# Block-sparse attention and a residual MLP on one core: four booked transfer times in the planner's order

## The chip, the core and the metric

The kernel runs on one core of a Trainium2 chip. The metric is the device time of one execution in microseconds (us). The version before has a median of 322.15 us in five runs (320.83 to 324.29). In the profile the engines are called PE (TensorE, matmuls), PEld (its weight loads), DVE (VectorE), ACT (ScalarE), POOL (GpSimd, here the issuer of loads) and SP (SyncE, the issuer of stores and of transposing transfers).

## What is computed

Attention over 4 batches, 8 heads, 768 positions and 64 elements a head, with a mask over blocks of 32 positions, then a residual MLP that mixes positions and then channels:

```python
scores = (q @ k.T) / sqrt(64)
mask = |bi - bj| <= 1, or block 0 or 23 on either side, or kb in sampled_blocks[qb]
attn = softmax(where(mask, scores, -1e9));  x = attn @ v      # (4, 768, 512)
a1 = alpha1 * x + beta1
u = x + lam * (w_tok @ a1)                                    # w_tok 768 x 768
a2 = alpha2 * u + beta2
out = u + lam * (relu(a2 @ w_ch1) @ w_ch2)                    # 512 -> 2048 -> 512
```

Inputs and output are float32; the kernel works in bf16 and f16 with float32 sums.

## The kernel before

**The work.** Two heads of a batch make a *pair*; there are 16, `p` = 0 to 15, four to a batch. A pair's scores are cut into nine *units* of 1024 columns. For the pairs 0 to 5 a unit is one group of QK matmuls on PE (L658), an exponential on ACT (L673) and PV matmuls (L698), with the mask inside the matmul as extra rows of q and k. For the pairs 6 to 15 two heads run side by side in QK (L736), the exponential is at L762, and VectorE applies the mask as a minimum with a table, `maskT` (L767), ahead of PV (L794). When a head's PV is complete, VectorE takes the reciprocal of the sums (L630) and multiplies (L633), which empties the PSUM bank `ops` and writes `x_sb`. For a pair follow: a1 on VectorE (L850 and L858, tile `a1p`), the position mixing on PE in two groups of 18 matmuls (L870, into PSUM tiles `mm`), its sum with x on VectorE (L880, which empties the `mm` bank), the product with alpha2 (L886, tile `ub`), and a transposition into `uT`: on PE (L907) for batch 0, by a transfer that SP issues (L917) for the others.

Once a batch's four `uT` are there, the channel part runs in eight half-batches `kk`: 16 groups of four matmuls with w_ch1 (L943, into `mm`), each with a relu on ACT (L954) or VectorE (L958) into `hts`, then three outputs of 16 matmuls with w_ch2 (L988, in groups of four, into `cp`, and near the end into `ops` too), an addition on VectorE (L1005), which empties `cp`, and a store on SP (L1012). There are two `mm` banks and, as long as attention lasts, one `cp` and one `ops`.

**Scaling of w2.** w_ch2 comes in four chunks of 512 KB (`load_w2`, L377) into `w2b`. The factor lam of the output is multiplied into it in place by eight VectorE instructions of 128x1024 (`sw`, L471), two to a chunk. Output matmuls L988 of the quarter `r` need the scalings 2r and 2r+1.

**The mask table.** VectorE makes 24 rows of it (L486), `mout` (L492) writes them out to a scratch tensor `mask_rows` in DRAM, each repeated 32 times, and `min_` (L495) reads the table back into `maskT`. Both transfers are issued on POOL, the second after the first is complete; both carry 1152 KB.

**Loads.** q, k and v of a pair are loads of 192 KB each on POOL (L308); VectorE casts q and k into `rel` (L508) and v into `vext` (L816). From pair 6 on SP then issues two transposing transfers (L597) that make `qx` and `kx`. From pair 8 on a pair's loads are held back: VectorE writes a *flag* (L324, `raise_flag`), POOL copies it (L306, `held`), and then issues q, k and v. The flag of pair p comes after the fourth unit of pair p - 2.

**What sets the order.** Each engine runs its instructions in program order, and that order is made when the program is built: a planner in the kernel holds every piece of work as a `Job` with a booked duration, a priority, dependencies and buffers taken and given. It goes through a clock of its own, gives each engine that is free the ready job of highest priority, emits its instructions, and books when it will be over. Loads leave in a fixed order by priority: those of pairs 0 to 6 with the other weights between, `mout`, two chunks of w2, `min_`, two chunks of w2, the pairs 7 to 15. A load's end is booked on one serial clock for transfers:

```python
if j.xfer is not None:
    dma_free[0] = max(dma_free[0], t + 2300.0) + j.xfer
    j.done = dma_free[0] + 200.0
```

and POOL takes no load while that clock is more than `AHEAD` = 13000 ns in front. Booked times decide the order alone; on the chip every instruction waits for what it really needs. At gaps in PE's plan before the first L988 the planner puts in matmuls on a dummy tile (L170, `keep_warm`).

Of the kernel before, what the change touches and what calls it, by code (L numbers as in the profile page):

```python
# [66 lines left out]
def kernel(  # L67
# [206 lines left out]
    def Copy(prio, fn, deps, take=(), give=()):  # L274
        j = Job(("ACT", "DVE"), 550.0, prio, fn, deps, take, give)
        j.alt = ACT_COPY
        return j
# [9 lines left out]
    def mmt(n, cols):  # L287
        return n * (max(cols, 60) / 2.4 + 2.7)
# [9 lines left out]
    def Load(xfer, prio, fn, deps=(), take=()):  # L298
        j = Job("POOL", 720.0, prio, fn, deps, take)
        j.xfer = xfer  # L300
        return j
# [12 lines left out]
    wload = {}  # L314
# [58 lines left out]
    def load_w2(g, prio, deps):  # L373
        def fn():
            if g == 0:
                w2tile.append(wk.tile([P, 16, DM], BF, name="w2b", tag="w2b", bufs=1))
            nc.gpsimd.dma_start(  # L377
                w2tile[0][:, 4 * g : 4 * g + 4, :],
                moe_w_ch2[ts(g, 4 * P), :].rearrange("(o p) n -> p o n", p=P),
            )  # L380

        wload["w2", g] = Load(2500.0, prio, fn, deps, ("w2b",) if g == 0 else ())

    order = iter(range(1000))
    load_pair(0, next(order))
# [16 lines left out]
    mout_prio = next(order)  # L402
    w2_prio = [next(order) for _ in range(2)]
    min_prio = next(order)
# [7 lines left out]
    for t in range(NT):  # L412
# [9 lines left out]
        j = Job("PE", mmt(NT, P), (5, t), tr, [wload["tok", t // 2]], take=("mm",))  # L422
# [4 lines left out]
    for g in range(4):  # L427
        load_w2(g, w2_prio[g], wtok_jobs)
# [19 lines left out]
    for g in range(4):  # L448
# [16 lines left out]
        j = Job("PE", mmt(16, 64), (5, 20 + g), bmm, [j_be2] + [wload["w1", i] for i in range(4)], take=("mm",))  # L465
# [32 lines left out]
        )  # L498

    j = Job("DVE", 400.0, (3, 3, 9), mrow, [wtok_jobs[-1]])  # L500
    j = Load(5000.0, mout_prio, mout, [j])
    mask_jobs = [Load(5000.0, min_prio, min_, [j])]

# [18 lines left out]
    for p in range(len(pairs)):  # L524
        if p == 0:
# [14 lines left out]
            j = Job("DVE", 720.0, (2, 0), fc)  # L540
            j = Job("PE", mmt(NT, P), (2, 0), f_tr, [j], take=("mm",))
            j = Copy((1, 0, 1), f_cq, [j, head_ready[0]], take=("head",))
            j = Copy((1, 0, 2), f_ck, [j], give=("mm", "rel"))
# [290 lines left out]
    for p in range(len(pairs)):  # L834
# [67 lines left out]
        if b == 0:  # L902
# [9 lines left out]
            j = Job("PE", mmt(NT, P), (2, p, 9), utr, ubs, take=("mm",), give=("ub",))  # L912
# [16 lines left out]
    for kk in range(2 * B):  # L929
        b, hf = divmod(kk, 2)  # L930
        relus = []
        for f in range(16):
# [18 lines left out]
            def rl(eng, kk=kk, f=f):  # L951
# [5 lines left out]
                else:  # L957
# [9 lines left out]
            deps = [ut_jobs[b * NPAIR + n] for n in range(NPAIR)] + b1_jobs  # L967
            take = ((("mm", "sps"), ("mmsel", kk, f)),) + (("hts",) if f == 0 else ())
            j = Job("PE", mmt(4, HS), (5, kk, f), c1, deps, take=take,
                    give=("uT",) if hf == 1 and f == 15 else ())  # L970
# [7 lines left out]
        for mi, (m, lo, w) in enumerate(parts):  # L978
            prev = last_m
            for r in range(4):  # L980
# [15 lines left out]
                deps = relus[4 * r : 4 * r + 4] + w2_jobs[2 * r : 2 * r + 2] + ([prev] if prev else [])  # L996
# [79 lines left out]
    while left:  # L1076
        moved = True
        while moved:
            moved = False
            for e in free_at:  # L1080
# [17 lines left out]
                j = best[1]  # L1098
# [47 lines left out]
        while events and events[0][0] <= t:  # L1146
            _, _, j = heapq.heappop(events)
# [45 lines left out]
```

## Time and profile before

| | |
|---|---|
| median of five runs | 322.15 us (320.83 to 324.29) |
| the profiled execution, its own time | 320.83 us |
| its span | 319.1 us |
| busy: PE, DVE, ACT, POOL | 308.0, 206.4, 208.6, 48.4 us |
| `mask_rows` written: issued, duration | 41.44, 12.2 us |
| `maskT` read: issued, duration | 54.24, 9.3 us |
| w2, four chunks: issued, median to landing | 42.66 to 55.5, 15.5 us |
| scaling of w2: first and last start, each | 58.2 and 74.9, 0.69 us |
| first L767 (uses `maskT`), first L988 (uses w2) | 78.3, 76.9 us |

How to read the lines: a timeline line has start, duration, engine, source line, operation, output and inputs with shapes, how many in a row, and in brackets how long the engine was idle before it and what ended that. A line of the waits has engine, tile and source line of the one that waited, then whom it waited for, then us in total, how often, and the longest. A line of the page's first part has engine, busy time, share of the span and number of instructions. A window's row gives each engine's busy time in that stretch; what it lacks of the stretch's length is idle.

### The profile page before, as it was taken

What the parts mean: (1) busy time and instruction counts of PE and PEld (TensorE: products, weight loads), DVE (VectorE), ACT (ScalarE), POOL (GpSimd) and SP (SyncE); (2) the same over time, 40 slices, a digit from 0 to 9 for tenths busy, and PEclk for the clock granted to TensorE, in tenths of its full rate; (3) what the DMA queues carried; (4) which work ended last, traced back from release to release, by engine and by line L of the source; (5) the groups of instructions that cost most, each with busy time, mean ns of one, the idle gap of its engine ahead of it and who ended that gap; (6) DMA issues with size and microseconds to landing.
All of it is one profiled execution on the core that took longest, in us unless ns stands there. A gap on an engine that the chain in (4) does not pass through costs nothing.

```text
span 319.1 us, 7783 instructions
## 1 busy us (share of the span) xinstructions
PE 308.0 (97%) x3308; PEld 192.9 (60%) x3340; DVE 206.4 (65%) x411; ACT 208.6 (65%) x267; POOL 48.4 (15%) x77
## 2 busy tenths in 40 slices
PE   7989999999999999999899999999999999999996
PEld 3777878775646566645555456645655575555544
DVE  4569977879868798867778797857877650201001
ACT  4989989897775678756675567746665526254630
POOL 4647141300203020202103020210000000000000
PEclk9999999999999999999999999999999999999999
DMA  6999999995533854190816634192010301201001
GB/s 149 177 229 206 215 218 192 261 171 99 75 76 67 146 103 78 42 183 35 123 27 113 137 52 85 48 128 89 2 27 33 92 3 25 100 2 61 38 28 72
DMA packets 46775, 31.97 MB, mean 100 GB/s; under 512 B 27516, under 2 KB 42264, under 8 KB 46612
## 3 DMA queue, kind: packets, MB, share of 16 engines
q0 software_dynamic: 16496, 17.83, 33.3%
q1 hardware_dynamic: 29992, 13.40, 18.1%
q8 instruction: 26, 0.43, 0.6%
q10 hardware_dynamic: 252, 0.24, 0.3%
q14 instruction: 9, 0.07, 0.1%
HBM read 32.04 MB, written 7.47 MB: 124 GB/s over the span
## 4 chain that ended last, share of the span: by engine, by line
PE 64%; DMA 19%; DVE 5%; issue 5%; POOL 4%; ACT 2%; POOLq 0%
PE mm L943 20%; PE cp L988 19%; PE ops L794 7%; PE sps L736 6%; DMA v<-in_v_dram 6%; PE mm L870 5%; DMA w2b<-in_moe_w_ch_dram 5%; DMA mask_rows<-maskT 4%; DMA k<-in_k_dram 4%; PE ops L988 4%; PE sps L943 2%; POOL q L308 1%; DVE eT L767 1%; DVE hts L958 1%; DMA q2f<-in_q_dram 1%
## 5 line engine op out<-in xcount | busy, mean ns | idle before, releaser
L762 ACT ACTIVATE eT<-sps 128x1024 f16<-128x1024 f32 x90 | 88.4, 1020 | 36.8 <-PE sps L736 35.0
L943 PE MATMUL mm<-uT,w1b 128*128 128x384 bf16 x472 | 90.3, 326 | 1.1 <-DVE x_sb L880 0.8
L954 ACT ACTIVATE hts<-mm,b1t 128x384 bf16<-128x384 f32 x96 | 55.8, 581 | 50.0 <-PE mm L943 47.5
L988 PE MATMUL cp<-w2b,hts 128*128 128x512 bf16 (+1 forms) x305 | 74.7, 373 | 1.8 <-DVE ot L1005 0.2
L943 PEld LDWEIGHTS <-w1b 128*128 128x128 bf16 x512 | 46.9, 97 | 35.3 <-issue 5.6
L767 DVE TENSOR_TENSOR eT<-eT,maskT 128x1024 f16<-128x1024 f16 x90 | 60.8, 686 | 8.8 <-ACT eT L762 8.5
L988 PEld LDWEIGHTS <-hts 128*128 128x128 bf16 x400 | 36.8, 98 | 34.0 <-issue 0.8
L673 ACT ACTIVATE eT<-sps 128x1024 f16<-128x1024 f32 (+1 forms) x55 | 52.4, 1013 | 5.1 <-PE sps L658 4.7
L1005 DVE TENSOR_TENSOR ot<-x_sb,cp 128x512 f32<-128x512 f32 (+1 forms) x21 | 14.1, 672 | 45.7 <-PE cp L988 45.7
L794 PEld LDWEIGHTS <-eT 128*128 128x128 f16 x720 | 29.2, 97 | 18.0 <-issue 4.5
L870 PE MATMUL mm<-a1p,wtokT 128*128 128x128 bf16 x576 | 36.7, 219 | 0.1
L794 PE MATMUL ops<-vext,eT 128*128 128x65 f16 x720 | 34.9, 194 | 0.5 <-DVE eT L767 0.5
L870 PEld LDWEIGHTS <-wtokT 128*128 128x128 bf16 x576 | 33.2, 98 | 1.7 <-issue 0.3
L658 PE MATMUL sps<-qx,kx 88*128 88x512 bf16 (+1 forms) x144 | 31.4, 325 | 0.9 <-ACT qx L231 0.5
L736 PE MATMUL sps<-qx,kx 64*128 64x512 bf16 (+1 forms) x240 | 27.3, 327 | 0.1
L306 POOL COPY held<-flag 1x1 bf16<-1x1 bf16 x8 | 4.3, 539 | 127.6 <-DVE flag L324 127.6
L698 PEld LDWEIGHTS <-eT 128*128 128x128 f16 x432 | 18.4, 97 | 5.5 <-DVE x_sb L633 1.7
L698 PE MATMUL ops<-vext,eT 128*128 128x65 f16 x432 | 20.5, 193 | 0.5 <-DVE x_sb L633 0.5
L880 DVE TENSOR_TENSOR x_sb<-x_sb,mm 128x384 f32<-128x384 f32 x32 | 17.5, 550 | 4.7 <-PE mm L870 4.5
L958 DVE TENSOR_SCALAR hts<-mm,b1t 128x384 bf16<-128x384 f32 x22 | 13.5, 615 | 8.9 <-PE mm L943 8.9
L633 DVE TENSOR_TENSOR x_sb<-ops,rcp 128x384 f32<-128x384 f32 x32 | 17.8, 558 | 1.1
L886 DVE TENSOR_TENSOR ub<-x_sb,a_bc 128x384 bf16<-128x384 f32 x32 | 17.5, 554 | 0.3
(73 smaller groups left out, 232.7 us busy)
## 6 DMA issues: line engine op xcount, KB each, us to landing
out_dram<-ot SPq DMA_DIRECT2D x23, 256.0 KB, 2.0
v<-in_v_dram POOLq DMA_DIRECT2D x16, 192.0 KB, 5.8
q<-in_q_dram POOLq DMA_DIRECT2D x15, 192.0 KB, 4.2
k<-in_k_dram POOLq DMA_DIRECT2D x15, 192.0 KB, 4.9
w1b<-in_moe_w_ch_dram POOLq DMA_DIRECT2D x4, 512.0 KB, 10.0
w2b<-in_moe_w_ch_dram POOLq DMA_DIRECT2D x4, 512.0 KB, 15.5
wtk<-in_moe_w_tok_dram POOLq DMA_DIRECT2D x3, 384.0 KB, 9.6
mask_rows<-maskT POOLq DMA_DIRECT2D x1, 1152.0 KB, 12.2
```

Source lines behind the costliest of these rows:

```text
L633: nc.vector.tensor_tensor(out=x_sb[:, s0 : s0 + NT, h * D : (h + 1) * D], in0=op[:, :, 0:D], in1=rcp[:].unsqueeze(2).broadcast_to([P, NT, D]),
L658: nc.tensor.matmul(sps[:, f - u * UN : f - u * UN + w], kx[h][0:KC, ts(jt, P)], qx[h][0:KC, c : c + w], start=True, stop=True,)
L673: nc.scalar.activation(eT[:, c], sps[:, c], AF.Exp, bias=EXPB, scale=SCALE)
L698: nc.tensor.matmul(ops[p, a][:, t * VW : t * VW + D + 1], eTs[p, u][:, ts(i - u * GU, P)], vx[:, a, jt, 0 : D + 1], start=(i % HT == 0), s ...
L736: nc.tensor.matmul(sps[:, a * 512 + lo : a * 512 + lo + w], kx[sl][r, ts(jt, P)], qx[sl][r, c : c + w], start=True, stop=True,)
L762: nc.scalar.activation(eT[:], sps[:], AF.Exp, bias=EXPB, scale=SCALE)
L767: nc.vector.tensor_tensor(out=e, in0=e, in1=maskT[:, u, :].unsqueeze(1).broadcast_to([P, 2, 512]), op=ALU.min,)
L794: nc.tensor.matmul(ops[p, a][:, t * VW : t * VW + D + 1], eTs[p, u][:, a * 512 + c * P : a * 512 + (c + 1) * P], vx[:, a, jt, 0 : D + 1], ...
L870: nc.tensor.matmul(tp[:, j, :], wtokT[:, s, ts(3 * g + j, P)], tl["a1p", p][:, s, :], start=(s == 0), stop=(s == NT - 1),)
L943: nc.tensor.matmul(hp[:, 0:HS], w1b[:, dk, ts(f, P)], uTs[b][:, dk, ts(hf, HS)], start=(dk == 0), stop=(dk == 3),)
L954: nc.scalar.activation(hts[kk][:, f, :], hp[:, 0:HS], AF.Relu, bias=b1t[:, f : f + 1], scale=1.0)
L988: nc.tensor.matmul(cps[kk, mi][:, 0:w], hts[kk][:, nk, ts(m, P)], w2tile[0][:, nk, lo : lo + w], start=(nk == 0), stop=(nk == 15),)
```

## The change

Four booked times of transfers in the planner are changed: a chunk of w2 from 2500 to 2900 ns, the last one to 4700; writing the mask's rows from 5000 to 7500; reading the table from 5000 to 3300. No instruction, dependency, buffer or priority is changed; the planner runs over the new times, and its order after them is another. The whole diff:

```diff
-        wload["w2", g] = Load(2500.0, prio, fn, deps, ("w2b",) if g == 0 else ())
+        wload["w2", g] = Load(4700.0 if g == 3 else 2900.0, prio, fn, deps, ("w2b",) if g == 0 else ())
...
-    j = Load(5000.0, mout_prio, mout, [j])
-    mask_jobs = [Load(5000.0, min_prio, min_, [j])]
+    j = Load(7500.0, mout_prio, mout, [j])
+    mask_jobs = [Load(3300.0, min_prio, min_, [j])]
```

In the built program POOL's order is the same before and after. VectorE's first differs at the first scaling of w2, which stood ahead of the addition L880 of the same stretch and now stands behind it; PE's first differs some 65 us into the span, where a group of L943 changes places with QK matmuls; SP's and ACT's differ from there on. The last L794 group of the attention part, and all that PE does after it, is in the same order in both.

## Prediction

> **What bounds the kernel now.** I read the page first, then the windows of 5 to 20 us, then TensorE's own waits, then VectorE's, and last the timeline around each TensorE wait.
>
> ```profile
> PE 308.0 (97%) x3308; PEld 192.9 (60%) x3340; DVE 206.4 (65%) x411; ACT 208.6 (65%) x267; POOL 48.4 (15%) x77
> ```
>
> TensorE (PE) is the bound: 308.0 of 319.1 us. Of the missing 11.1 us, 3.3 lie at the very end (the window 300 to 319.1 has 15.84 busy), which nobody disputes below. The windows from 60 to 260 us together lack 3.9 us. A change of order that leaves TensorE's work alone can therefore give back some 4 us at most; what it can lose has no such end. What those waits are:
>
> ```profile
> PE mm L943 <- DVE x_sb L880: 0.8, 1, 0.8
> PE ops L794 <- DVE eT L767: 0.5, 1, 0.5
> PE ops L698 <- DVE x_sb L633: 0.5, 2, 0.3
> PE cp L988 <- DVE ot L1005: 0.2, 1, 0.2
> ```
>
> Five waits of TensorE between 58 and 260 us, all for VectorE (DVE). Each really costs 0.16 more than shown, since a group's end is modelled (one L943 matmul is listed at 326 ns, while eight take 1.30 us in the chain, a step of 162). So: 0.33 at 62.21, 0.45 at 72.42, 1.0 at 157.31, 0.70 at 194.73, 0.41 at 212.84. And why VectorE was late:
>
> ```profile
> 60.76 0.69 DVE L471 TENSOR_TENSOR w2b<-w2b,lam_bcb 128x1024 bf16<-128x1024 bf16 x1 [0.76 <-DMA w2b<-in_moe_w_ch_dram]
> 61.59 0.56 DVE L633 TENSOR_TENSOR x_sb<-ops,rcp 128x384 f32<-128x384 f32 x1
> 70.97 0.69 DVE L471 TENSOR_TENSOR w2b<-w2b,lam_bcb 128x1024 bf16<-128x1024 bf16 x1 [0.58 <-DMA w2b<-in_moe_w_ch_dram]
> 71.80 0.56 DVE L633 TENSOR_TENSOR x_sb<-ops,rcp 128x384 f32<-128x384 f32 x1
> ```
>
> The first two waits: a scaling of w2 (L471) stands in VectorE's queue before its chunk has landed, and the normalization behind it (L633), which frees TensorE's `ops` bank, is late. The other three have another cause:
>
> ```profile
> DVE rel L508 <- DMA q<-in_q_dram: 5.2, 7, 1.2
> DVE rel L508 <- DMA k<-in_k_dram: 3.4, 3, 1.7
> DVE vext L816 <- DMA v<-in_v_dram: 3.2, 4, 1.5
> ```
>
> From 76 us on VectorE waits 11.8 us for the q, k and v of pairs 8 to 15, and what stands behind the cast waits too:
>
> ```profile
> 149.48 0.06 DVE L324 MEMSET flag<- 1x1 bf16 x1
> 154.30 0.36 DVE L508 COPY rel<-q 128x768 bf16<-128x768 bf16 x1 [0.67 <-DMA q<-in_q_dram]
> 155.32 0.36 DVE L508 COPY rel<-k 128x768 bf16<-128x768 bf16 x1 [0.20 <-DMA k<-in_k_dram]
> 156.43 0.36 DVE L816 COPY vext<-v 128x768 f16<-128x768 f16 x1 [0.28 <-DMA v<-in_v_dram]
> 156.70 0.55 DVE L880 TENSOR_TENSOR x_sb<-x_sb,mm 128x384 f32<-128x384 f32 x1
> 157.31 0.81 PE L943 MATMUL mm<-uT,w1b 128*128 128x384 bf16 x4 [0.84 <-DVE x_sb L880]
> ```
>
> Pair 12: flag, three late casts, then the add L880 that empties an `mm` bank, then the matmuls that wanted the bank.
>
> **The change part by part.** It alters four booked transfer times in the planner and no instruction. The order of the instructions shows:
>
> *Same work.* TensorE has the same matmuls and the same 118 fillers in both orders, POOL the same queue in the same order. One relu goes from ScalarE (ACT) to VectorE (0.58 there, 0.62 here; both are 65% busy): nothing. TensorE's order is equal up to some 65 us and again from the last L794 group, some 256 us, to the end. So start and tail cost nothing, and all is decided by TensorE's waits in between.
>
> *The scalings of w2 (8 x 0.69 us).* They move back past one L880, two normalizations, two L886 and a cast. Chunk 0 had landed by 58.24, chunk 1 by 60.76, chunk 2 by 67.69, chunk 3 by 70.97, and the new places are all behind these times: the first behind the L880 at 59.45, the third and fourth behind or beside the copy of uT near 64.7, the fifth behind both L850 and L858, the seventh behind the L880 that comes after the normalization. VectorE's 2.2 us of waiting for w2 go. With them go the 0.33 and 0.45 of TensorE: at 61.4 the normalization follows the L880 and one scaling with no DMA wait; at 71.6 it comes ahead of the scaling, and TensorE now has an L870 group (1.00) and two QK matmuls (0.43) in front of its need. **-0.8 us** (bounds: 0, if VectorE's idle 1.5 us before the L880 at 59.45 only shifts the lateness; -0.8, all of it). Who uses w2: the first L988 at 76.9 needs scalings 0 and 1, over by 64; the last quarter is wanted near 94, scaled by 76. Covered by over 15 us. The mask's first use, 78.3, comes after the table has landed (54.24 plus 9.3); covered too.
>
> *The loads of pairs 8 to 15.* Everything behind 76 us is re-dealt. The POOL queue has the same rule (flag, then q, k, v), so I take the landing after the flag from the casts that waited in the trace: q 3.8 to 5.9, mean 4.5 (seven); k 5.84, 5.87, 6.24, mean 6.0; v 8.66, 6.48, 6.95, 7.76, mean 7.5. Against it stands VectorE's work between flag and cast, by steps from the timeline (L767 0.60, L880 and L886 0.47, L850 and L858 0.87, L958 0.54, L1005 0.60, cast 0.28). In us, q / k / v, before -> after: pair 8, 2.7/5.1/5.4 -> 2.8/3.6/6.5; 9, 3.1/6.0/6.3 -> 5.8/6.6/8.9; 10, 4.9/5.5/5.2 -> 5.3/7.6/5.6; 11, 2.6/2.9/5.5 -> 2.9/3.2/7.2; 12, 3.5/4.2/5.0 -> 3.5/3.8/7.1; 13, 2.9/6.9/7.2 -> 3.5/4.2/4.5; 14, 4.9/5.5/5.2 -> 2.7/3.6/6.3; 15, 2.6/2.9/5.5 -> 3.1/6.0/6.3. Shortfalls (a first wait counted as cover for the next cast): before 18.4 us in all, of which the trace shows 11.8; after 16.0. So VectorE waits no more than before. What differs is what stands behind the late cast:
>
> Pairs 9, 10, 15: nothing of TensorE's close behind, or covered: 0 (pair 10: up to 0.5, a relu behind v). Pairs 12, 14 and 15 lose their present 1.0, 0.70 and 0.41: **-2.1**.
> Pair 8: k (short 2.4 in all) stands straight before an L880; behind the second L870 group TensorE has one L943 group (0.65), then wants the bank. That is pair 12's shape of today, where 1.15 of waiting gave 1.0. I take 1.3 (0 to 2.0).
> Pairs 11 and 12: k before L880, and the `min` L767 that the next L794 needs; cover one L988 group (0.86). Shape of pair 14 today: 0.7 each (0 to 1.2).
> Pair 14: k before L880; cover one L870 group and an L794: 1.0 (0 to 1.5).
> Pair 13: q, k and v all ahead of the L1005 that frees `cp`; in pair 15 today that L1005 began 6.5 us after its flag and cost 0.41; here, behind v, 7.7: 1.0 (0 to 1.6).
> Sum **+4.7**.
>
> *Queues passed.* SP's transposes (L597) follow the casts and are late by as much, but a flag comes 15 units ahead of its pair, at 17.9 us a pair (flags from 80.4 to 205.6) some 30 us: covered. Stores and L917 change places on SP; `ot` has two buffers, a store lands in 2.0: covered.
>
> Sum: -0.8 - 2.1 + 4.7 = +1.8 on the profiled execution's 320.83 us (span 319.1 and 1.7 around it), 322.6. The median of the runs, 322.15, stands 1.3 above that execution: 324.0.
>
> The row for a load of q, k or v is 4.2, 4.9 and 5.8 us from issue to landing. The Trainium skill ("DMA: Bandwidth & Descriptors", "Anatomy of one DMA — SWDGE (gpsimd) path") puts a GpSimd load at about 2.0 us plus its bytes over 436 GB/s, by my estimate 2.5 us for 192 KB; with that nearly every cast would find its data, and the sum would be -2.9, 319.3 on the median. The rows say otherwise, and decide.
>
> **The rivals.** *Absorbed (not slower).* VectorE's waits pass on to TensorE in the share of today, 2.1 of 11.8. With 16.0 for 18.4 of shortfall that is 1.8: -0.3 and -0.8, so 321.1. For it: pair 11 today waits 2.39 and TensorE loses nothing; against it: the shapes named above. It decides if the L943 and L988 groups in front of the need last longer than the wait.
> *Waits gone (not slower).* No late cast reaches TensorE: -0.8 - 2.1, 319.3. Against it: six pairs keep q or k closer than the data.
> *Later landings (slower by over a percent).* The loads land at the late end of the rows, v 8.66 and k 6.24. Pair 13 pays 1.2 more, pair 10 1.2 (its relu then holds a bank), four k's 0.26 each: +3.4, 327.4. It decides from v past 8.
> *No effect.* Excluded: the orders differ on four engines.
>
> **How the numbers follow.** Chances: forecast 0.50 (its own range 322.3 to 325.8), absorbed 0.27, waits gone 0.07, later landings 0.16. One percent of 322.15 is 3.2 us, about what a measurement of this kernel can tell from no change. Slower by more, over 325.4: later landings and a quarter of the forecast, 0.29. Faster by more, under 318.9: only the best of waits gone, 0.05. Range 320.2 (absorbed, less its uncertainty of 0.9) to 327.4.
>
> **What would show it.** Right: no wait of L471 for w2; the two L698 waits near 62 and 72 gone; TensorE waiting at L943 or L794 for L880 or L767 some 7 us behind the flags of pairs 8, 11, 12 and 14, and at L988 for L1005 in pair 13; nothing behind pairs 9 and 15. Windows from 60 to 260 lacking 5.7 us in place of 3.9. Wrong: TensorE waits for ScalarE, or `held` copies on POOL come later and shift the landings, or the re-dealt order leaves TensorE without a ready bank where no load is near.

## The result, and the profile after

| | before | after |
|---|---|---|
| median of the runs beside each other | 322.57 us (320.29 to 327.05, 76 runs) | 326.11 us (322.80 to 334.96, 39 runs) |
| profiled execution, its own time | 320.83 us | 323.86 us |
| its span | 319.1 us | 322.1 us |

The changed kernel takes 1.0081 times as long, with a 95% interval of 1.0061 to 1.0101: slower, by some 2.6 us. Executions over 1.5% above the fastest of their kernel, most of them at a lowered granted clock, are left out of every ratio here, and after has more of them, so the medians of all runs lie further apart than the ratio; the profiled executions of e2, e3 and e6 ran at a clock of 0.99, so no span of theirs is compared.

The page's first line of after:

```profile
PE 308.3 (96%) x3310; PEld 192.6 (60%) x3340; DVE 206.9 (64%) x412; ACT 207.8 (65%) x266; POOL 50.3 (16%) x77
```

The work of each engine is what it was: PE 308.3 us for 308.0, VectorE 206.9 for 206.4. Of the 3.0 us of span 2.7 are idle time of PE. Where it lies, by the windows from 60 to 262 us (start and end, length, then the busy time of PE, PEld, DVE, ACT and POOL, the granted clock, the share of the DMA engines, GB/s), first of before, then of after:

```profile
60.00:262.00 202.00, 198.08 (x2156) 119.33 (x2181) 156.01 (x299) 134.92 (x170) 20.84 (x32) 1.00 0.48 85
```

```profile
60.00:262.00 202.00, 194.89 (x2103) 115.94 (x2126) 155.61 (x296) 132.94 (x168) 22.60 (x32) 1.00 0.49 84
```

In 202 us PE lacks 3.92 before and 7.11 after, 3.2 more at the same clock. That is the whole loss of this pair of executions, and it lies in the attention stretch. Some 1.3 us of either number are no waiting: the traces of before and after hold 289 and 291 records of the 320 output matmuls L988 of 128x512 into `cp`, and where a record is missing PE seems idle. (The traces of e8, e10 and e11 hold all 320, and there L988 has no idle time but for a wait that is named.) What PE waited for in after are six waits of 5.6 us in place of five of 2.1. The two at L698 for the normalization are gone. The six in PE's timeline of after:

```profile
85.84 0.81 PE L943 MATMUL mm<-uT,w1b 128*128 128x384 bf16 x4 [1.35 <-DVE x_sb L880]
...
139.52 0.29 PE L794 MATMUL ops<-vext,eT 128*128 128x65 f16 x4 [0.35 <-DVE eT L767]
...
157.51 0.30 PE L794 MATMUL ops<-vext,eT 128*128 128x65 f16 x4 [1.36 <-DVE eT L767]
...
179.20 1.02 PE L988 MATMUL cp<-w2b,hts 128*128 128x512 bf16 x4 [1.42 <-DVE ot L1005]
...
195.10 0.30 PE L794 MATMUL ops<-vext,eT 128*128 128x65 f16 x4 [0.56 <-DVE eT L767]
195.94 0.81 PE L943 MATMUL mm<-uT,w1b 128*128 128x384 bf16 x4 [0.55 <-DVE x_sb L880]
```

They stand behind the flags of the pairs 8 (79.09), 11 (132.26), 12 (149.37), 13 (170.00) and 14 (188.56, two waits). VectorE, meanwhile, waits for its loads hardly longer than before, from 76 to 260 us:

```profile
DVE rel L508 <- DMA q<-in_q_dram: 6.2, 6, 2.5
DVE rel L508 <- DMA k<-in_k_dram: 4.2, 4, 1.6
DVE vext L816 <- DMA v<-in_v_dram: 2.3, 2, 1.4
```

12.7 us for 11.8, in 12 waits for 14. The same waiting of VectorE costs PE some three times as much (5.6 us shown, for 1.6 without the two waits for the scalings). The reading is that other instructions stand behind it. VectorE in after, at pair 13:

```profile
170.00 0.06 DVE L324 MEMSET flag<- 1x1 bf16 x1
...
174.78 0.36 DVE L508 COPY rel<-q 128x768 bf16<-128x768 bf16 x1 [0.20 <-DMA q<-in_q_dram]
...
176.41 0.36 DVE L508 COPY rel<-k 128x768 bf16<-128x768 bf16 x1 [0.80 <-DMA k<-in_k_dram]
178.19 0.36 DVE L816 COPY vext<-v 128x768 f16<-128x768 f16 x1 [1.42 <-DMA v<-in_v_dram]
178.46 0.68 DVE L1005 TENSOR_TENSOR ot<-x_sb,cp 128x512 f32<-128x512 f32 x1
```

q lands 4.8 us behind the flag, k 6.4, v 8.2. The sum that empties `cp` stands behind all three, and the matmuls at 179.20 wait for it.

### The profile page after: what moved, and what is told of

The parts are those of the page before. It is cut to its first block, busy times and chain, and to the rows that moved or that the text cites. A ratio compares the mean times of both kernels' runs of the same rounds, so it can differ in the third digit from the quotient of the medians.

```text
span 322.1 us, 7786 instructions
## 1 busy us (share of the span) xinstructions
PE 308.3 (96%) x3310; PEld 192.6 (60%) x3340; DVE 206.9 (64%) x412; ACT 207.8 (65%) x266; POOL 50.3 (16%) x77
## 4 chain that ended last, share of the span: by engine, by line
PE 75%; DMA 10%; DVE 6%; POOL 4%; ACT 3%; issue 2%; ACTq 0%
PE mm L943 21%; PE cp L988 18%; DMA k<-in_k_dram 8%; PE mm L870 7%; PE ops L794 7%; PE sps L736 6%; PE sps L658 5%; PE ops L988 4%; PE ops L698 3%; PE sps L943 2%; DMA v<-in_v_dram 2%; POOL q L308 1%; DVE eT L767 1%; POOL held L306 1%; DMA q2f<-in_q_dram 1%
## 5 line engine op out<-in xcount | busy, mean ns | idle before, releaser
L943 PE MATMUL mm<-uT,w1b 128*128 128x384 bf16 x472 | 90.4, 326 | 2.1 <-DVE x_sb L880 1.9
L988 PE MATMUL cp<-w2b,hts 128*128 128x512 bf16 (+1 forms) x307 | 75.7, 374 | 2.9 <-DVE ot L1005 1.4
L943 PEld LDWEIGHTS <-w1b 128*128 128x128 bf16 x512 | 46.9, 97 | 34.9 <-issue 5.5
L767 DVE TENSOR_TENSOR eT<-eT,maskT 128x1024 f16<-128x1024 f16 x90 | 60.8, 686 | 10.3 <-ACT eT L762 10.2
L988 PEld LDWEIGHTS <-hts 128*128 128x128 bf16 x400 | 36.5, 97 | 35.6 <-issue 2.8
L1005 DVE TENSOR_TENSOR ot<-x_sb,cp 128x512 f32<-128x512 f32 (+1 forms) x21 | 14.1, 673 | 46.2 <-PE cp L988 45.9
L794 PEld LDWEIGHTS <-eT 128*128 128x128 f16 x720 | 29.5, 97 | 19.9 <-DVE eT L767 7.2
L794 PE MATMUL ops<-vext,eT 128*128 128x65 f16 x720 | 35.5, 194 | 2.3 <-DVE eT L767 2.3
L306 POOL COPY held<-flag 1x1 bf16<-1x1 bf16 x8 | 6.2, 771 | 131.4 <-DVE flag L324 131.4
L880 DVE TENSOR_TENSOR x_sb<-x_sb,mm 128x384 f32<-128x384 f32 x32 | 17.6, 551 | 9.1 <-PE mm L870 9.0
L698 PEld LDWEIGHTS <-eT 128*128 128x128 f16 x432 | 18.5, 97 | 4.6 <-DVE x_sb L633 0.2
L698 PE MATMUL ops<-vext,eT 128*128 128x65 f16 x432 | 20.4, 193 | 0.0
L958 DVE TENSOR_SCALAR hts<-mm,b1t 128x384 bf16<-128x384 f32 x23 | 14.2, 616 | 7.4 <-PE mm L943 7.4
L736 PEld LDWEIGHTS <-kx 64*128 64x128 bf16 x240 | 8.2, 94 | 15.7 <-issue 13.2
```

Source lines behind the costliest of these rows:

```text
L698: nc.tensor.matmul(ops[p, a][:, t * VW : t * VW + D + 1], eTs[p, u][:, ts(i - u * GU, P)], vx[:, a, jt, 0 : D + 1], start=(i % HT == 0), s ...
L736: nc.tensor.matmul(sps[:, a * 512 + lo : a * 512 + lo + w], kx[sl][r, ts(jt, P)], qx[sl][r, c : c + w], start=True, stop=True,)
L767: nc.vector.tensor_tensor(out=e, in0=e, in1=maskT[:, u, :].unsqueeze(1).broadcast_to([P, 2, 512]), op=ALU.min,)
L794: nc.tensor.matmul(ops[p, a][:, t * VW : t * VW + D + 1], eTs[p, u][:, a * 512 + c * P : a * 512 + (c + 1) * P], vx[:, a, jt, 0 : D + 1], ...
L943: nc.tensor.matmul(hp[:, 0:HS], w1b[:, dk, ts(f, P)], uTs[b][:, dk, ts(hf, HS)], start=(dk == 0), stop=(dk == 3),)
L988: nc.tensor.matmul(cps[kk, mi][:, 0:w], hts[kk][:, nk, ts(m, P)], w2tile[0][:, nk, lo : lo + w], start=(nk == 0), stop=(nk == 15),)
```

## The experiments

The theory: casts of held loads (L508, L816) stand in VectorE's queue before their data have landed, at places where an instruction that gives PE a bank or its next input is queued behind them; in after these places cost more than in before. The rivals: the moved scalings cost it, the transfers of the mask table cost it, or it is the order of PE itself. A wait of PE is given below as its line shows it in brackets, without the 0.16 that the prediction adds. Spans of single executions differ by a start as well. At one L698 near 54 us, before the first instruction whose place the change alters, PE stands up to 2.8 us in some of them, and the profile shows nothing that it waits for; e7 has

```profile
54.81 0.58 PE L698 MATMUL ops<-vext,eT 128*128 128x65 f16 x14 [1.60 <-issue]
```

e1 has 1.03 there, e5 1.52, e8 2.20, and e2, e3 and e6 2.3 to 2.8; before, after, e4, e9, e10 and e11 have none.

### One half of the change at a time: e1 and e2

e1 has only the line of w2's booked times of the change, e2 only the two lines of the mask table's.

> Only the booked times of w2 are changed (2900, last chunk 4700); those of the mask stay at 5000. The order that comes out moves the scalings of w2 much as the whole change does, but from the flag of pair 9 on (some 99 us) it is the order of before again, with the casts of pairs 11 to 14 where before had them. Theory (late casts of pairs 8 and 11 to 14 cost the time): the two waits near 62 and 72 us lose most of their 0.8, the waits of 1.0, 0.7 and 0.4 in pairs 12, 14 and 15 stay, so 320.0 to 320.8, 3 us below the whole change. Rival (the moved scalings of w2 themselves cost it): 323 or more, as with the whole change.

> Only the booked times of the two mask transfers are changed (7500 and 3300); w2 stays at 2500 a chunk. The order differs from before until the flag of pair 10 (some 114 us) and is the order of before after it. Theory: 320.0 to 321.0, since pairs 11 to 14 stand as before; pair 8 has its casts 5.7, 6.0 and 8.0 us of work behind its flag and should cost nothing. Rival (any new order around the mask and w2 costs some us by itself): 322.5 to 324.

e1: 0.9981 (0.9943 to 1.0020) of before, span 319.9. The scalings move as in after, the two early waits are gone, but from pair 9's flag on the order is that of before, and so are the places of three waits: 1.10 at L943 in pair 12, 0.30 at L794 in pair 14, 0.58 at L988 in pair 15. A fourth, 0.72 at L794 in pair 8, is its own. The profiled execution took 321.69 us, 0.9 more than the 320.0 to 320.8 that were expected; the start has 1.03 of that. So the moved scalings as such cost nothing that these runs can tell.

e2: 0.9963 (0.9914 to 1.0012). From pair 10's flag on the order is that of before. Its waits, at the lower clock, are 1.23 at L943 in pair 12, 0.55 at L794 in pair 14, 0.29 at L988 in pair 15, and a new 1.35 at L988 in pair 11, where the same order had none in before. Its profiled execution took 327.08 us at that clock, which cannot be held against the 320.0 to 321.0 expected; the ratio lies as near to 1 as was expected.

Neither half makes the kernel slower. The loss belongs to the order of the pairs 8 to 14 that only the two together give.

### Late casts moved behind what waits for them: e5 and e10

The order of after, but on VectorE the casts of some pairs are issued three pieces of work later. e5: pairs 8 and 11 to 14. e10: pair 13 alone.

```diff
+    later = {casts[p, nm].n: 3 for p in (8, 11, 12, 13, 14) for nm in "qkv"}
...
-                j.out = j.fn(e) if len(j.eng) > 1 else j.fn()
+                emit(j, e)
```

`emit` keeps a job listed in `later` back until that many further pieces of VectorE's work are issued, and with it whatever depends on it. In e10 the list of pairs is `(13,)`.

> The order of the changed kernel on every engine, except that the casts of q, k and v of the pairs 8, 11, 12, 13 and 14 are issued three VectorE instructions later; loads, flags and all else unchanged. Theory (what stands behind the late cast is the cost): TensorE's waits of 1.35, 0.35, 1.36, 1.42 and the pair of waits near 192 go or shrink below 0.5 each; 323.9 falls by 4 to 5.5 to some 319. VectorE goes on waiting for loads, a little less. Rival (the waits come from the re-dealt order at large, or from the loads landing late as such): 322.5 to 324, the waits move to other lines.

> The order of the changed kernel, except that the casts of pair 13 alone are issued three VectorE instructions later, behind the L1005 that frees the cp bank. Theory: TensorE's wait of 1.42 (1.58 with the modelled end) at L988 near 179 us goes, the other places keep theirs; span 322.1 falls to some 320.5. Rival (order at large, or a shared cause of the waits): 322, and a wait of the size comes back elsewhere.

e5: 0.9875 (0.9815 to 0.9936, from five executions), span 317.8 for 322.1. Of PE's waits from 58 to 262 us one is left:

```profile
PE ops L794 <- DVE eT L767: 0.2, 1, 0.2
```

PE lacks 1.76 us in the window from 60 to 262 in place of 7.11, that is 5.4 less; 1.3 of the 1.76 are again records of L988 that are missing. And pair 13 on VectorE of e5:

```profile
168.78 0.06 DVE L324 MEMSET flag<- 1x1 bf16 x1
...
175.29 0.69 DVE L1005 TENSOR_TENSOR ot<-x_sb,cp 128x512 f32<-128x512 f32 x1 [1.35 <-PE cp L988]
...
176.48 0.35 DVE L508 COPY rel<-q 128x768 bf16<-128x768 bf16 x1
```

The sum L1005 begins 6.5 us behind the flag (in after 8.5) and now waits for PE and not the other way round. The cast, 7.7 us behind the flag, finds its data. This is the theory's strongest test: the work and the loads are those of after, and only the place of 15 casts differs, with the transposes behind them. One thing was not as expected: VectorE's waiting for loads does not go down a little, it falls from 12.7 us to 1.3 (both in pair 15). So e5 shows that the late casts are the cause, but not by itself that it matters what stands behind them. For that stand the two orders, where nearly the same waiting cost PE 1.6 and 5.6 us, and pair 15 of after, where q and v are 0.7 and 0.9 late and PE does not wait.

e10: 1.0010 (0.9976 to 1.0045), span 320.4 for 322.1. Pair 13's wait is gone, as this line of PE's timeline shows, which has no bracket:

```profile
177.64 1.03 PE L988 MATMUL cp<-w2b,hts 128*128 128x512 bf16 x4
```

The others stay, 1.46 in pair 8, 1.01 in pair 12, 0.52 and 0.47 in pair 14; pair 11's, which was not moved, did not come up this time. The two that are missing were 1.42 and 0.35, and the span is shorter by 1.7. So the wait at L988 is the doing of pair 13's casts, and it did not come back elsewhere; the span and the time of e10 hold pair 11's missing wait as well.

### The flag taken away: e3 and e4

POOL's copy of the flag is dropped in after (e3) and in before (e4), so that the loads of pairs 8 to 15 leave as soon as their buffers are free:

```diff
-                nc.gpsimd.tensor_copy(out=held_[0:1, held : held + 1], in_=flag[0:1, held : held + 1])
+                pass
```

> The order of the changed kernel, but POOL does not copy the flag ahead of the loads of pairs 8 to 15 (the copy has no part in the result), so q, k and v leave as soon as their buffers are free, long before their casts. Theory: VectorE's 12.7 us of waiting for these loads go, and TensorE's five late places with them: 323.9 falls by 5 to 6, to some 318. Rival (order at large): 323 to 324 with TensorE's waits still there. A second rival: the early loads collide with the other transfers, the uT and qx/kx transpositions land later, and new waits take part of the gain.

> The same for the order of before: no copy of the flag on POOL. Theory: the waits of 1.0, 0.7 and 0.4 in pairs 12, 14 and 15 go, 320.8 falls by 2.1 to 318.7, and before and after without the hold stand within 1 us of each other, after lower by the 0.8 of the w2 scalings. Rival (order at large): the gap of 3 us between the two orders stays.

e3: 0.9853 (0.9783 to 0.9923, from four executions). From 76 us on VectorE has no wait for a load, and PE none at all from 58 to 262. e4: 0.9919 (0.9875 to 0.9963), span 317.9; the waits of the pairs 12, 14 and 15 are gone, 0.29 at L698 and 0.53 at L943 near the scalings (72.20 and 76.73 us) remain, and 0.2 for a transposition. With the data there in time, the order of after is not slower than that of before: the two ratios' intervals overlap. The order of PE itself is no cause. The second rival, early loads that collide with other transfers, shows itself only in that 0.2 of e4.

### The loads booked later: e8 and e9

In after (e8) and in before (e9) the planner books the held loads with more time, so that it places their casts later itself:

```diff
-                    dma_free[0] = max(dma_free[0], t + 2300.0) + j.xfer
+                    dma_free[0] = max(dma_free[0], t + j.lead) + j.xfer
```

`lead` is 3500 for pairs from 8 on and 2300 for all others, and their `xfer` 1300 in place of 980.

> The changed booked times, and the loads of pairs 8 to 15 booked as late as the trace shows them (lead 3500, 1300 each). The w2 scalings stand behind their data, and the casts 2.6 to 8.3, 5.2 to 9.4 and 5.4 to 9.1 us of work behind the flag. Theory: both kinds of waits go, span 316.5 to 318.5, not slower than the same booking without the change. Rival (the change brings a loss of its own by another way): 319 or more.

> Before, but the planner books the loads of pairs 8 to 15 as late as the trace shows them (lead 3500 in place of 2300, 1300 in place of 980 each: q, k and v some 5.0, 6.3 and 7.6 us behind the flag). The casts come out 4.4 to 6.6, 5.1 to 9.7 and 5.5 to 9.9 us of work behind the flag, but for q of pairs 11 and 15 at 2.6. Theory: most waits on loads go, TensorE's 2.1 shrink below 1, 319 to 320. Rival (a new order has new places of its own kind): 321 to 324.

e9: 0.9915 (0.9874 to 0.9955), span 317.3. What is left of PE's waits in e9 are two near the early scalings (72.06 and 76.33 us):

```profile
PE ops L698 <- DVE x_sb L633: 0.4, 1, 0.4
PE mm L943 <- DVE x_sb L880: 0.3, 1, 0.3
```

e8: 0.9897 (0.9834 to 0.9959), span 318.6, with no PE wait from 58 to 262. (The span is 0.1 above what was expected, and 2.2 of it are the standstill at L698 near 54 us, where before and after have none.) VectorE still waits 1.9 us for loads in e8, and none of it reaches PE. Booking nearer to the measured landing is the cheap remedy, and it needs no order by hand.

### The early scalings alone: e6, e7 and e11

In before the third, fifth and seventh scaling are issued one piece of VectorE's work later (e6); the same with the casts of the pairs 12, 14 and 15 three later (e7); the same with the bookings of e9 (e11).

```diff
+    later = {w2_jobs[g].n: 1 for g in (2, 4, 6)}
```

> The order of before, except that three scalings of w2 are issued one VectorE job later: the third behind the normalization, the fifth behind L858, the seventh behind the next normalization. Theory: the two waits of TensorE near 62 and 72 us go, 0.8 less: 320.0 beside 320.8, all else equal to before. Rival (that lateness is only shifted, since exponentials bound that stretch): 320.8.

> The order of before with the three later scalings of w2 and the casts of pairs 12, 14 and 15 three VectorE instructions later. Theory: 0.8 and 2.1 go, 318.0, the fastest of the held orders. Rival (a cast moved back makes its own successor late): 319.5 to 321.

> Before with the loads of pairs 8 to 15 booked late, and three scalings of w2 one VectorE job later. Without the second the profile shows a span of 317.3, with waits of TensorE of 0.40 near 72 and 0.27 near 76 us behind a late scaling. Theory: these go, span 316.5 to 317. Rival (the lateness of that stretch is only shifted): 317.3.

e6: 0.9991 (0.9948 to 1.0034), which tells nothing of 0.8 us by the time alone. Both L698 waits are gone, but in this execution, at the lower clock, the later places all pay more than in before, and one that paid nothing there pays most:

```profile
145.38 1.02 PE L988 MATMUL cp<-w2b,hts 128*128 128x512 bf16 x4 [1.98 <-DVE ot L1005]
```

That is pair 11, whose k landed 7.97 us behind its flag, where it took 5.87 in before and PE had no wait.

e7: 0.9949 (0.9911 to 0.9986), span 320.3; the profiled execution took 322.06 us, where 318.0 had been expected, a miss by 4 us. Of these, 1.60 are the standstill near 54 us. The waits of before are gone or small, as expected (0.17 is left in pair 12), but others came in their place. PE's waits in e7:

```profile
PE cp L988 <- DVE ot L1005: 1.1, 1, 1.1
PE mm L943 <- DMA uT<-ub: 0.7, 1, 0.7
PE ops L794 <- DVE eT L767: 0.2, 1, 0.2
```

The first is pair 11 again, on VectorE of e7:

```profile
141.32 0.36 DVE L508 COPY rel<-k 128x768 bf16<-128x768 bf16 x1 [2.77 <-DMA k<-in_k_dram]
```

Its k landed 7.09 us behind the flag. In before this pair, which e7 does not move, had no wait with its k at 5.87. The second wait, 0.66 at 203.85 us, is likely the edit's own: pair 14's casts, now later, bring its transposes to SP at 196.81 and 198.27 us, right ahead of `uT` at 199.60, which left at 197.77 in before. That was not tried by itself.

e11: 0.9899 (0.9859 to 0.9940), span 316.5, no PE wait from 58 to 262, and PE lacks 0.40 us of the 202 (its trace has all records of L988). VectorE still waits 3.0 us for loads, but with late bookings no landing reaches PE in this trace, and the two waits near the scalings, which e9 still had, are gone too. Against e9 the span is 0.8 shorter, which is the size of those two waits; the two ratios do not tell them apart (0.9899 and 0.9915).

e3, e4, e5, e8, e9 and e11 all beat both kernels, by 0.8 to 1.5% against before, and e7 by 0.5%. The intervals of the six overlap, so none is called the fastest; e3, e8 and e11 are those whose traces show no wait of PE in that stretch.

## Why the prediction was nearly right

**What held.** The bound, the mechanism and the sign. The windows say that PE's idle time between 60 and 262 us is the whole difference, the six waits stand at the places that were named, and e5 and e3 show that VectorE's late casts of held loads make them. The ratio makes 324.8 us of the prediction's basis of 322.15, where 324.0 stood. On the profiled execution the forecast was 322.6, and it took 323.86: 3.0 us more than before, where 1.8 had been forecast. The range, 320.2 to 327.4, reached from one rival to another, so the time alone would not have told them apart; the places do. The 4 us that the prediction called the most to be won are less, since 1.3 of them are missing records; e11, which has no wait left, is 2.6 us shorter in span than before.

**Term by term** (the measured waits are the bracket and 0.16, as the prediction counts them):

| term | forecast, us | in after, us |
|---|---|---|
| early scalings, 62 and 72 us | -0.8 | -0.78, both gone |
| pairs 12, 14, 15 as in before | -2.1 | -2.11, all gone |
| pair 8 | 1.3 | 1.51 |
| pair 11 | 0.7 | 0.51 |
| pair 12 | 0.7 | 1.52 |
| pair 13 | 1.0 | 1.58 |
| pair 14 | 1.0 | 1.43 |
| pairs 9, 10, 15 | 0 | 0 |
| net | +1.8 | +3.66 |

By the brackets alone PE's waits grew by 3.5 (2.09 to 5.59), its idle time in the window by 3.2, the span by 3.0. What the brackets leave of the window's idle time is 1.8 in before and 1.5 in after, mostly the missing records; and in the first 60 us PE was busy 0.4 longer in after.

**The terms that were too small: 12, 13 and 14,** by 0.8, 0.6 and 0.4. The step that failed is the landing after the flag, taken as one mean each for q, k and v (4.5, 6.0, 7.5). In pair 13 v came at 8.2, and L1005 began 8.5 us behind the flag where 7.7 had been reckoned. In pair 12, on VectorE of after:

```profile
149.37 0.06 DVE L324 MEMSET flag<- 1x1 bf16 x1
...
156.02 0.36 DVE L508 COPY rel<-k 128x768 bf16<-128x768 bf16 x1 [1.63 <-DMA k<-in_k_dram]
156.30 0.55 DVE L880 TENSOR_TENSOR x_sb<-x_sb,mm 128x384 f32<-128x384 f32 x1
156.76 0.69 DVE L767 TENSOR_TENSOR eT<-eT,maskT 128x1024 f16<-128x1024 f16 x1
```

k came 6.65 us behind the flag, and PE wanted the `min` at the end of that queue: 0.65 late by the load. That is most of the 0.8, and more than the bound of 1.2 allowed. In pair 14 q came at 5.5 in place of 4.5, and a `min` L767 stood between the casts of q and k: PE waited there for 0.56 and then for the add L880 for 0.55. The prediction's sum had only the second place, and k as the late one, which did not wait. On VectorE and POOL of after:

```profile
188.56 0.06 DVE L324 MEMSET flag<- 1x1 bf16 x1
190.24 0.71 POOL L308 DMA_DIRECT2D q<-in_q_dram  x1 [1.10 <-issue]
194.08 0.36 DVE L508 COPY rel<-q 128x768 bf16<-128x768 bf16 x1 [2.49 <-DMA q<-in_q_dram]
```

This lateness was to be had from the trace of before: there too POOL issued this q 1.69 us behind its flag, later than any other pair's, and it landed at 5.87, the latest of the seven that made the mean of 4.5. In the mean over the waiting casts of after q took 4.7, k 6.2 and v 8.4 us (two), each later than the means used (of v only those above some 7 us show, since earlier ones find no cast waiting).

**The rivals.** *Absorbed* took PE's loss as a fixed share of VectorE's waiting, 2.1 of 11.8. It fell: VectorE waits 12.7, and PE loses 6.6 (5.6 in brackets and six times 0.16). That VectorE's total is about the same was forecast, and it decides nothing. *Waits gone* fell with six waits. Its price in the prediction was also what a figure of the Trainium skill led to ("DMA: Bandwidth & Descriptors", "Anatomy of one DMA — SWDGE (gpsimd) path"; by my estimate 2.5 us a load). In after the page's rows have 3.8, 5.2 and 6.2 us for q, k and v from issue to landing, and those decide. *Later landings* came in half: v did pass 8 us (8.2 in pair 13, 8.7 in pair 15), but pair 13 paid 0.6 more and not 1.2, and pairs 10 and 15 nothing.

**What is only argued.** That it takes both halves of the change to reach the new order was seen, not explained: which booking tipped which choice of the planner was not followed.

## What to carry to other kernels

Read a late load by what is queued behind the instruction that waits for it: 12 us of VectorE's waiting cost the matmul engine 2.1 us in one order and 6.6 in another (with the 0.16 a wait), and moving 15 copies of 0.36 us three pieces of work back took away all of it but 0.4. Where a planner books transfers, book those that have a dependent close by at their late end (here some 1.2 us more lead and 0.3 more transfer gained 0.85% on before), since a place that holds in one execution can fail in the next. And do not forecast a reordering with mean landings: the cost begins at the cover and only counts upwards, so the spread alone makes the sum larger. What a pair's own row shows, as q of pair 14 did, goes before the mean.

## What the runs showed of the hardware that was not expected

The same load at the same place of the same order lands at quite different times. k of pair 11 behind its flag, in runs whose order around it is that of before: 5.87 us in before, 5.98 in e1, 7.09 in e7, 7.34 in e2, 7.97 in e6 (the last two at a granted clock of 0.99, the others at 1.00). PE's wait at the L988 behind it: none, none, 1.09, 1.35, 1.98. In all five POOL issues this k 1.32 or 1.33 us behind the flag, so the difference lies between issue and landing. What makes it was not isolated. In this stretch SP's transposing transfers of `rel` and `ub` run at the same time (in e7 `uT` from 137.38 and `qx` from 138.69 us, with k's cast at 141.32; in before `uT` from 136.80 and `qx` from 138.69, with the cast at 139.53); no run took them away alone, so the cause stays open.

What lies ahead of the loads repeats, in contrast. From the flag to the issue of q POOL takes 0.36 to 1.04 us, and the value belongs to the place in the order and not to the execution: for pair 11 it is 0.63 or 0.64 in before, e1, e2, e6, e7 and e9, and 0.92 in after, e5 and e10. For pair 14 it is 1.67 to 1.69 in all eleven traces that have the flag's copy, with 1.10 to 1.36 us in which POOL waits for nothing that the profile shows.
